# Short convolution in eight steps of sixteen channels, the skip term as a column, row pairs in the last product, and a new order of all work

## The chip, the cores and the metric

The kernel runs on one core of a Trainium2 chip. A core has five engines that work at the same time: TensorE (PE) multiplies matrices and writes the sums to PSUM, VectorE (DVE), ScalarE (ACT) and GpSimd (POOL) work on vectors, SyncE (SP) mostly issues transfers. They meet only at semaphores. PSUM has eight banks of 128 x 512 float32; whatever PE writes has to be moved to SBUF by DVE or ACT ("evacuated") before the bank can be used again.

The metric is the time of the program on the device in microseconds. A profiled execution gives a span, from the first to the last instruction, and its own time, which is a little longer.

## The reference, cut to what matters

Sequence S = 2048, width D = 640, hidden width F = 1728, all in bfloat16.

```
x  = A_q
q  = layernorm(x)
k_shift[s, d] = sum over t < 4 of k[s - t, d] * shift_k[d, t]      # short convolution
kv = k_shift * v
y  = causal_convolution(kv, ssm_k)                                # length S, by FFT
y  = y + kv * ssm_D                                               # skip term
h  = x + q * y
a  = mish(layernorm(h) @ w1 + b1)
h2 = h + a @ w2
```

The skip term is the same as adding ssm_D to the first tap of the long filter: the convolution with ssm_k[d, 0] + ssm_D[d] at lag 0 gives both.

## The kernel before, in words

**Tiling.** The 2048 positions lie as 128 partitions x 16 positions (p, t2) in memory; the long convolution is a transform written as matrix products. The width is cut into five blocks b of 128 channels, and these into chunks 0 (blocks 0, 1), 1 (blocks 2, 3) and 2 (block 4).

**Stages.** Names are those of the order list; a trailing x or y is the first or second half of a unit (one PSUM bank each).

- *k1pe/k1ev* (L625): the long filter ssm_k, loaded by channel rows into rn, is transposed block by block, 16 transposes each, and evacuated into kk_s. *dadd* (L620) then adds ssm_D to the first tap, which is 128 elements in one partition row; d_row is a row of ssm_D in the partition 0 of rn.
- *s1kpe/s1kev* (L543, L544): first transform of the filter. Cosine and sine products of 64 output rows each run on the two halves of the array's columns.
- *coef, wsh* (L487, L493, L501): the short filter. One matmul with a 0/1 matrix (rep4) copies shift_k to all partitions, four copies move it into coef with a shift per group of 32 partitions, and four products on POOL with a mask of 32 columns make banded matrices of 128 + 96 columns for each of 20 channel groups of 32.
- *ktpe/ktev* (L571): k is transposed, four channels groups by four time steps of 32 channels per unit; *ktsh* (L585) copies the last time group moved by one column.
- *kspe/kv* (L595, L596, L600): the short convolution. For each channel group and each group of four steps there are two products: 128 columns for the group itself and 96 for what the group before hands over. DVE multiplies the sum with v on the way out of PSUM.
- *s1vpe/s1vev*: first transform of kv, as for the filter.
- *s2kpe, s2vpe* (L652, L685): second transform, one matmul per frequency, with the table G (4 MB, eight loads d_g). Evacuated in place.
- *sw* (L668, L669): copies of the transformed filter with neighbouring partitions exchanged, in two halves of 64 frequencies per chunk; SP issues them.
- *p1, p2* (L706, L710): complex products of kv's and the filter's transforms, in quarters of 32 frequencies.
- *i1pe, i2p, y*: inverse transforms and their evacuation; *ln1, lnx, wb, h, bn, pow, hc*: the two layernorms and the gating; *trpe, trd*: transposes of the normalised rows.
- *m1pe* (L898), *hb* (L903): first product of the MLP in five units of 256, 256, 512, 512, 512 positions, 13 hidden blocks of 128, Mish on ACT. *m1pex* (L878): the last 64 hidden rows, two groups of positions on the two halves of the array, into the two halves of hbx.
- *m2pe* (L915, L916), *res* (L921), *d_out*: second product, 13 matmuls of 128 rows and a last one (L916) whose 128 rows hold the 64 of this group of positions and 64 that meet zeros (w2z and w2h_z, L760 and L761, write these zeros on POOL).
- *wm* and *fz* (L464, L468): matmuls on zeros, at the start and at four places later.

**Order.** ORDER lists all 1030 operations with their engine (t TensorE, a ScalarE, v VectorE, p GpSimd, d and s transfers issued by SP and ACT). _schedule walks this list, gives each operation a start by a cost model of its own and assigns PSUM banks; the program is emitted in the order of these starts. Each engine, and each queue of transfers, then works strictly in that order, and waits by semaphores where data or a buffer is missing. DVE and GpSimd products that use the same port are kept from overlapping in this plan, and a small copy (turn, L936) makes GpSimd wait where it follows DVE.

The functions the diff touches, and what calls them:

## Time and profile before

| | |
|---|---|
| three runs | 224.22, 224.60, 224.79 us, median 224.6 |
| profiled execution, own time | 224.86 us |
| its span | 223.1 us |
| granted TensorE clock | 1.00 |
| busy PE | 214.7 us (96%), 2598 matmuls |
| busy DVE, ACT, POOL | 146.2, 134.4, 65.7 us |
| DMA | 30.68 MB; 408 to 424 GB/s while the inputs load |

"Busy" of PE counts a matmul from its start to its modelled end; since matmuls are pipelined, a matmul of 128 columns counts about 0.22 us although the next can start 0.056 us later. So a busy share near 100% does not say that PE runs at its pace: that is read from how many matmuls start in a stretch. "Idle before" in a group's line is the time that an engine had nothing, with what ended it. A line such as L419 or L421 is the helper that all evacuations use.

### The profile page before, as it was taken

The numbers are of one execution on the slowest core, as the hardware profiler recorded it, in microseconds if no ns is written. First come the engines' busy times: TensorE is split into PE (matmuls) and PEld (weight loads), VectorE is DVE, ScalarE is ACT, GpSimd is POOL, SyncE is SP. The second block draws the span as 40 slices with busy tenths as digits, with TensorE's granted clock in tenths as the row PEclk, the third lists the DMA queues.
The fourth block names the chain that finished last, engine by engine and source line by source line (L and its number), as shares of the span: only waits on it lengthen the run. The fifth ranks groups of instructions, "written<-read, shape, count | busy, mean of one in ns | idle before, by whom it ended". The sixth has DMA issues, their size and how long they took to land.

```text
span 223.1 us, 6218 instructions
## 1 busy us (share of the span) xinstructions
PE 214.7 (96%) x2598; PEld 162.1 (73%) x2598; DVE 146.2 (66%) x317; ACT 134.4 (60%) x268; POOL 65.7 (29%) x106
## 2 busy tenths in 40 slices
PE   7998899999999999999999999999999999999994
PEld 2988899999877999988887644576645445675773
DVE  0699989999999998999788898974400000004023
ACT  2689989999999999888870446800053454330000
POOL 1271950005596007235767714320000000000000
PEclk9999999999999999999999999999999999999999
DMA  6999991075999999100001401043350000000024
GB/s 214 388 408 424 408 413 69 3 203 193 277 290 283 319 351 347 62 3 0 3 0 32 88 0 31 0 91 60 88 179 0 1 0 3 0 0 0 32 82 153
DMA packets 27342, 30.68 MB, mean 138 GB/s; under 512 B 9393, under 2 KB 23730, under 8 KB 26930
## 3 DMA queue, kind: packets, MB, share of 16 engines
q1 hardware_dynamic: 26880, 30.10, 41.1%
q8 instruction: 20, 0.33, 0.6%
q10 hardware_dynamic: 338, 0.18, 0.3%
q14 instruction: 8, 0.07, 0.1%
q0 software_dynamic: 96, 0.00, 0.0%
HBM read 20.45 MB, written 2.62 MB: 103 GB/s over the span
## 4 chain that ended last, share of the span: by engine, by line
PE 64%; DVE 13%; DMA 7%; ACT 7%; POOL 5%; issue 2%; SPq 0%; DVEq 0%; ACTq 0%; POOLq 0%
PE ps L915 21%; PE ps L898 19%; ACT uv L419 6%; DMA x<-in_A_q_dram 5%; PE ps L743 4%; PE ps L744 4%; PE ps L652 3%; PE ps L543 2%; PE ps L571 2%; DMA rn<-in_A_ssm_k_dram 2%; DVE st L776 2%; DVE st L822 2%; PE ps L595 2%; POOL r L782 2%; PE ps L916 2%
## 5 line engine op out<-in xcount | busy, mean ns | idle before, releaser
L915 PE MATMUL ps<-rn,uv 128*128 128x320 bf16 (+2 forms) x416 | 61.1, 299 | 0.2 <-DVE x L921 0.2
L903 ACT ACTIVATE uv<-ps,b1s 128x512 bf16<-128x512 f32 (+1 forms) x65 | 35.4, 610 | 39.1 <-PE ps L898 38.5
L898 PE MATMUL ps<-G 128*128 128x512 bf16 (+1 forms) x325 | 58.6, 337 | 0.0
L915 PEld LDWEIGHTS <-uv 128*128 128x128 bf16 x416 | 40.2, 98 | 17.5 <-issue 0.4
L419 ACT CAST uk<-ps 128x512 bf16<-128x512 f32 (+1 forms) x96 | 48.7, 702 | 2.6 <-PE ps L544 1.6
L898 PEld LDWEIGHTS <-G 128*128 128x128 bf16 x325 | 31.2, 98 | 23.9 <-issue 1.1
L921 DVE TENSOR_TENSOR xb<-ps,xb 128x320 bf16<-128x320 f32 (+2 forms) x12 | 5.7, 487 | 36.3 <-PE ps L916 35.8
L419 ACT CAST uv<-ps 128x512 bf16<-128x512 f32 (+2 forms) x57 | 28.7, 845 | 0.0
L921 DVE TENSOR_TENSOR xa<-ps,xa 128x320 bf16<-128x320 f32 x12 | 5.9, 488 | 21.6 <-PE ps L916 21.6
L827 POOL TENSOR_TENSOR r<-ve,mhalf 128x1 f32<-128x1 f32 x16 | 10.0, 630 | 32.7 <-DVE ve L824 32.7
L743 PE MATMUL ps<-a,uv 128*128 128x128 bf16 x160 | 18.8, 219 | 0.2
L421 DVE CAST uk<-ps 128x512 bf16<-128x512 f32 (+1 forms) x27 | 17.2, 669 | 1.4 <-PE ps L744 0.9
L743 PEld LDWEIGHTS <-uv 128*128 128x128 bf16 x160 | 17.9, 113 | 0.0
L421 DVE CAST uv<-ps 128x512 bf16<-128x512 f32 (+1 forms) x25 | 15.3, 677 | 0.0
L685 PE MATMUL ps<-uv,G 128*128 128x64 bf16 (+1 forms) x256 | 12.8, 197 | 0.8
L685 PEld LDWEIGHTS <-G 128*128 128x128 bf16 x256 | 11.1, 96 | 3.1 <-issue 2.1
L600 DVE TENSOR_TENSOR ra<-ps,rb 128x512 bf16<-128x512 f32 x20 | 12.5, 684 | 0.3 <-PE ps L596 0.3
L419 ACT CAST rb<-ps 128x512 bf16<-128x512 f32 (+1 forms) x28 | 10.6, 495 | 2.7 <-PE ps L803 2.7
L652 PE MATMUL ps<-uk,G 128*128 128x160 bf16 x128 | 12.1, 230 | 0.0
L782 POOL TENSOR_TENSOR r<-ve,mhalf 128x1 f32<-128x1 f32 x16 | 10.8, 672 | 1.3
L706 DVE TENSOR_TENSOR uv<-uv,uk 128x2048 bf16<-128x2048 bf16 (+1 forms) x11 | 10.9, 1022 | 0.0
L544 PE MATMUL ps<-cst,ra 128*64 128x128 bf16 x160 | 10.6, 220 | 0.1
(116 smaller groups left out, 376.7 us busy)
## 6 DMA issues: line engine op xcount, KB each, us to landing
G<-tab_g SPq DMA_DIRECT2D x8, 512.0 KB, 12.9
rn<-in_A_ssm_k_dram SPq DMA_DIRECT2D x5, 512.0 KB, 6.2
ra<-in_A_k_dram SPq DMA_DIRECT2D x4, 640.0 KB, 9.9
rb<-in_A_v_dram SPq DMA_DIRECT2D x2, 1280.0 KB, 13.1
G<-in_B_w_dram SPq DMA_DIRECT2D x5, 432.0 KB, 6.4
rn<-in_B_w_dram SPq DMA_DIRECT2D x1, 2080.0 KB, 9.8
rn<-uk SPq DMA_DIRECT2D x4, 512.0 KB, 5.1
rb<-uk SPq DMA_DIRECT2D x8, 256.0 KB, 7.9
```

The lines of the kernel that those rows point to most:

```text
L419: nc.scalar.copy(o, i)
L421: nc.vector.tensor_copy(o, i)
L600: nc.vector.tensor_tensor(kv_w[:, m, :, 8 * h:8 * h + 8, l0:l0 + n], ps.rearrange("p (l t d) -> p d t l", l=n, t=8), raw_v[:, 8 * h:8 * h ...
L652: nc.tensor.matmul(ps[:, o:o + 160], g_v[:, f, :], KA[:, :, f, :], start=True, stop=True)
L685: nc.tensor.matmul(ps[:, fl * n:fl * n + n], g_v[:, f0 + h * kf + fl, :], VX[x][:, :, f0 + h * kf + fl, :], start=True, stop=True)
L706: eng.tensor_tensor(v, v, K[c.i][:, :, f0:f1, :], ALU.mult)
L743: nc.tensor.matmul(pz[:, k, :], V[c.i][:, dg // 4, :, dg % 4], a12[:, 0, :], start=True, stop=False)
L782: nc.gpsimd.tensor_tensor(r1[:, t2:t2 + 1], ve1[:, t2:t2 + 1], mhalf[:, 0:1], ALU.pow)
L898: nc.tensor.matmul(ph[:, 0:w], w1[:, dc, fc * P:fc * P + P], lnhT_of(u)[:, dc, 0:w], start=(dc == 0), stop=(dc == NDC - 1))
L903: nc.scalar.activation(hb_of(u)[:, fc, 0:w], rt.tile[:, 0:w], ACT.Mish, bias=b1s[:, fc:fc + 1], scale=1.0)
L915: nc.tensor.matmul(po[:, 0:d1 - d0], hb_of(u)[:, fc, tl * P:(tl + 1) * P], w2[:, fc, d0:d1], start=(fc == 0), stop=False)
L921: nc.vector.tensor_tensor(x, rt.tile[:, 0:d1 - d0], x, ALU.add)
```

## The change

- **Short convolution.** Groups are now 16 channels by 8 time steps (128 rows again). A unit has the same eight matmuls, but the second of each pair has 48 columns, not 96; even and odd channels of a group of 32 go to every second column of the PSUM bank. The shifted coefficients are made by nine accumulating matmuls with parts of the identity as weights, evacuated by one copy on ACT; ten products on POOL, each 704 columns, make the banded matrices. The shift of the last time group is 8 x 127 elements instead of 4 x 127.
- **Skip term.** ssm_D comes as a column of five bfloat16 per partition (d_col): block 0 on ACT's queue, blocks 1 to 4 by four transfers of POOL. DVE adds a column of 128 x 1 to the raw filter (dq0 to dq4) ahead of the transposes of the first half. dadd and d_row are gone.
- **First filter block.** Its upper 64 rows are loaded by ACT, the lower by SP, and it is first. On ACT's queue the order is: half block, cst, d_col, sk_r.
- **Row pairs.** The last 64 rows of m2pe are a unit of their own, m2q: for two groups of positions and two parts of the output, products of 64 rows on the upper or the lower half of the array start the sums of four banks. The zeros (w2z, w2h_z) are gone. m1pex pairs the two halves of each unit.
- **Pieces.** The swap copies of chunk 0 go in four pieces of 32 frequencies, its products in eight of 16.
- **Fillers.** wm has eight matmuls, not nine; each fz two, not one, all four at places after the first transforms of v.
- **Order.** All 1052 operations stand in a new order. For PE it begins wm, k1pe0y, k1pe0x, cfpe, k1pe2y, k1pe2x, then s1kpe0. Loads are five filter blocks, k with d_x0 in it, a12, then v among the first table parts, then the rest of the table. In PE's order there are 58 changes between full-array matmuls and those on a half of it, where there were 28.

The core of the diff (the order list, constants of the planner and tile shapes are left out):

```diff
     def emit_act_dmas(e):
+        nc.scalar.dma_start(raw_n[0][64:P], n_view[0, 16:32])
         nc.scalar.dma_start(cst[:], dram["cst"])
-        nc.scalar.dma_start(sk_r[:], A_shift_k.rearrange("(d n) j -> d (n j)", n=20))
-        nc.scalar.dma_start(d_row, A_ssm_D.unsqueeze(0))
+        nc.scalar.dma_start(d_col[:, 0:1], d_view[0])
+        nc.scalar.dma_start(sk_r[:], A_shift_k.rearrange("(d n) j -> d (n j)", n=40))
+    def emit_dp(e):
+        for m in range(1, NDC):
+            nc.gpsimd.dma_start(d_col[:, m:m + 1], d_view[m])
...
-        nc.tensor.matmul(ps_f32(cf_rt)[:, 0:80], rep4, sk_r[:], start=True, stop=True)
+        ps = ps_f32(cf_rt)[:, 0:440]
+        for i, (a, j0, j1) in enumerate(((0, 0, 4), (4, 0, 4), (7, 1, 4), (7, 0, 1), (1, 0, 4), (2, 0, 4), (3, 0, 4), (5, 0, 4), (6, 0, 4))):
+            nc.tensor.matmul(ps.rearrange("p (r t) -> p r t", t=11)[:, :, a + j0:a + j1], cst[0:16, 3 * P - 16 * a:4 * P - 16 * a],
+                             sk_r[:].rearrange("p (r j) -> p r j", j=4)[:, :, j0:j1], start=(i == 0), stop=(i == 8))
...
-        for a in range(4):
-            ps = slice(a * 32, a * 32 + 32)
-            nc.vector.tensor_copy(coef[ps, :, a:a + 4], cf_rt.tile[ps, 0:80].rearrange("p (g j) -> p g j", j=4))
+        ev(e, coef[:], cf_rt.tile[:, 0:440])
...
-            nc.gpsimd.tensor_copy(t[:, :, 4, 1:128], t[:, :, 3, 0:127])
+            nc.gpsimd.tensor_copy(t[:, :, 2, 1:128], t[:, :, 1, 0:127])
...
-                for l in (2 * k, 2 * k + 1):
-                    r = 4 * m + l
-                    for a in (2 * h, 2 * h + 1):
-                        o = ps[:, (l - 2 * k) * 256 + (a - 2 * h) * P:][:, 0:P]
-                        nc.tensor.matmul(o, t[:, l, a, :], wsh[r // 5][:, r % 5, 0:128], start=True, stop=False)
-                        nc.tensor.matmul(o[:, 0:96], t[:, l, a - 1 if a else 4, :], wsh[r // 5][:, r % 5, 128:224], start=False, stop=True)
+                for l in range(2):
+                    for e in range(2):
+                        o, q, w = ps[:, 256 * l + e:256 * l + 256:2], 4 * e + 2 * k + l, wsh[m][k][:, e, l, :]
+                        nc.tensor.matmul(o, t[:, q, h, :], w[:, 0:128], start=True, stop=False)
+                        nc.tensor.matmul(o[:, 0:48], t[:, q, 0 if h else 2, :], w[:, 128:176], start=False, stop=True)
...
-        def dadd(e, kd=kd, rd=rd):
-            k = kd[0:1, 0]
-            (nc.vector if e == "dve" else nc.gpsimd).tensor_tensor(k, k, rd, ALU.add)
+        def dadd(e, n=n, b=b):
+            nc.vector.tensor_tensor(n[:, 0:1], n[:, 0:1], d_col[:, b:b + 1], ALU.add)
+        k1 = OP(f"dq{b}", ("dve", 0.1), [d_n[b], d_rows if b else d_row1], emit=dadd)
...
-        npf = (32, 32, 32)[len(c.dcs) - 1]
+        npf = (16, 32, 32)[c.i]
...
+            def pq(e, ab=ab, parts=parts):
+                for i in range(2):
+                    for t2 in ab:
+                        _, c, h = last64[t2]
+                        d0, d1, rt = parts[t2][i]
+                        rhs = w2h[64:P, d0:d1] if h else w2[0:64, 13, d0:d1]
+                        nc.tensor.matmul(ps_f32(rt)[:, 0:d1 - d0], hbx[64 * h:64 * h + 64, c:c + P], rhs, start=True, stop=False)
...
                     for fc in range(NFC - 1):
-                        nc.tensor.matmul(po[:, 0:d1 - d0], hb_of(u)[:, fc, tl * P:(tl + 1) * P], w2[:, fc, d0:d1], start=(fc == 0), stop=False)
-                    nc.tensor.matmul(po[:, 0:d1 - d0], lhs, w2h[:, d0:d1] if h else w2[:, 13, d0:d1], start=False, stop=True)
+                        nc.tensor.matmul(po[:, 0:d1 - d0], hb_of(u)[:, fc, tl * P:(tl + 1) * P], w2[:, fc, d0:d1], start=False, stop=(fc == NFC - 2))
```

More of the change, by code (lines that the diff above doesn't have):

```diff
@@ L187, in _schedule @@
         dur = dict(o.opts)[eng]
-        est = max([free.get(eng, 0.0)] + [d.finish + d.lat + _TAIL[d.eng] + _HOP for d in o.deps])
+        est = max([free.get(eng, 0.0)] + [d.finish + (0.0 if d.eng == eng and eng.startswith("dma") else d.lat + _TAIL[d.eng] + _HOP) for d in o.deps])
         base = est
@@ L191, in _schedule @@
             t, rt.slot = rt.ring.free()
+            rt.ring.take(rt.slot, rt)
             est = max(est, t)
@@ L204, in _schedule @@
                     t = fetched
-                fetched = t + (_SLOW if free.get("dma", 0.0) > t + 0.3 else _FETCH)
+                fetched = t + next(d for end, d in _FETCH if t < end)
                 mark += _BLOCK
@@ L215, in _schedule @@
                 o.behind = last
-        for rt in o.allocs:
-            rt.ring.take(rt.slot, rt)
         order.append(o)
@@ L327 @@
     turn = cpool.tile([P, 1], BF16, name="turn")
[L328 to L329 removed]
+    sk_r = cpool.tile([16, 160], BF16, name="sk_r")
+    d_col = cpool.tile([P, NDC], BF16, name="d_col")
+    coef = cpool.tile([P, 440], BF16, name="coef")
     st1 = cpool.tile([P, NT, 2, 6], F32, name="st1")
@@ L530 @@
     d_go = OP("d_go", ("dma", 0.75))
-    d_n = [DMA(f"d_n{b}", P * S * 2, emit_kn(b), deps=[d_go], lat=3.1) for b in range(NDC)]
+    d_n = [DMA("d_n0", P * S * 2, emit_kn(0), deps=[d_go], rate=405e3, lat=2.85)]
+    d_n += [DMA(f"d_n{b}", P * S * 2, emit_kn(b), deps=d_n[:1], rate=405e3, lat=3.2) for b in range(1, NDC)]
+    for o in d_k + d_v:
+        o.deps.append(d_n[0])
     s1_pes = [[] for _ in CHUNKS]
```

289 lines of the change are left out of this document (148 added, 141 removed).

## The prediction

> **What bounds the kernel now.** The profiled execution took 224.86 us around a span of 223.1 us; the median of the three runs is 224.6. I sum against 224.86 and take 0.26 off at the end.
>
> I read the table by stretches first: columns are the stretch, its length, busy us and instruction count of PE, PEld, DVE, ACT, POOL, then granted clock, DMA share, GB/s.
>
> ```profile
> 7.00:30.00 23.00, 21.10 (x489) 20.13 (x489) 20.98 (x43) 19.72 (x35) 14.26 (x18) 1.00 1.03 413
> 30.00:50.00 20.00, 20.00 (x420) 19.43 (x418) 19.95 (x34) 20.00 (x44) 1.49 (x3) 1.00 0.43 145
> 50.00:72.50 22.50, 20.95 (x464) 18.29 (x462) 22.34 (x32) 22.50 (x49) 14.94 (x9) 1.00 0.90 259
> 72.50:92.00 19.50, 19.41 (x319) 18.87 (x317) 17.70 (x31) 18.89 (x40) 4.67 (x8) 1.00 0.92 309
> 92.00:223.00 131.00, 127.82 (x895) 82.86 (x892) 64.67 (x178) 51.29 (x102) 29.31 (x58) 1.00 0.14 36
> ```
>
> There are two regimes. From 72.5 us on PE is never idle until the last outputs, and its matmuls come at a fixed pace: PE alone sets the end there. Before 72.5 us DVE and ACT are full (42.29 and 42.50 of 42.5 us from 30 on), because they empty PSUM; PE waits for them although it looks 95% busy, since a matmul's latency (about 0.2 us) covers the pauses. Between 7 and 30 us both evacuators have holes: 2.02 us on DVE, 3.28 on ACT, while the loads run at 413 GB/s.
>
> The chain of waits gives the paces and one pause of PE for "issue" (nothing that the profile shows):
>
> ```profile
> 26.93 0.83 issue
> 51.02 0.96 PE ps L685 x32
> 143.13 1.77 PE ps L915 x13
> 144.90 0.14 PE ps L916
> ```
>
> So a 320-column matmul costs 0.136 us and a 64-column one 0.03. The timeline of PE shows how much the pauses hide, what a short-convolution pair costs, and what a change of array form costs:
>
> ```profile
> 7.01 1.21 PE L625 MATMUL ps<-cst,rn 128*128 128x128 bf16 x16
> 8.15 0.24 PE L543 MATMUL ps<-cst,rb 128*64 128x128 bf16 x1
> 9.24 0.22 PE L544 MATMUL ps<-cst,rb 128*64 128x128 bf16 x1
> 9.39 3.23 PE L625 MATMUL ps<-cst,rn 128*128 128x128 bf16 x48
> 42.01 0.22 PE L595 MATMUL ps<-xb,uv 128*128 128x128 bf16 x1
> 42.06 0.20 PE L596 MATMUL ps<-xb,uv 128*128 128x96 bf16 x1
> 42.10 0.22 PE L595 MATMUL ps<-xb,uv 128*128 128x128 bf16 x1
> 60.65 2.51 PE L685 MATMUL ps<-uv,G 128*128 128x64 bf16 x56
> ```
>
> At 60.65 us 56 matmuls take 2.51 us where 0.03 each would be 1.68: PE waits for evacuated banks. A pair L595+L596 takes 0.10 us. From full-array to half-array matmuls (the last L625 starts at 7.01 + 1.21 - 0.22 = 8.00) and back (9.24 to 9.39) the step is 0.15 us instead of 0.06: about 0.1 us per switch, 0.11 with the slower first matmul behind it.
>
> The groups by shape (busy us, mean ns) give the prices off PE:
>
> ```profile
> L706 DVE TENSOR_TENSOR uv<-uv,uk 128x2048 bf16<-128x2048 bf16 x7 | 8.3, 1215 | 0.0
> L706 DVE TENSOR_TENSOR uv<-uv,uk 128x1024 bf16<-128x1024 bf16 x4 | 2.7, 685 | 0.0
> L493 DVE CAST coef<-ps 32x80 bf16<-32x80 f32 x4 | 1.0, 240 | 0.0
> L824 DVE TENSOR_SCALAR ve<-mv 128x1 f32<-128x1 f32 x16 | 2.5, 153 | 0.6
> L501 POOL TENSOR_TENSOR xb<-cst,coef 128x1120 bf16<-128x1120 bf16 x3 | 6.2, 2065 | 0.5 <-DVE coef L493 0.5
> L585 POOL COPY uv<-uv 128x508 bf16<-128x508 bf16 x5 | 3.0, 610 | 1.1 <-DVE uv L421 1.1
> ```
>
> **The change part by part.**
>
> *Evacuators (the bound before 72.5 us).* DVE loses the four coefficient casts (0.96), the memset of coef (0.18) and one skip add (0.21). Of the chunk-0 products it had six at 1.22 us (7.3); the new order has sixteen half-sized ones, nine on POOL, seven on DVE at 0.685 (4.8): -2.5. One chunk-2 product goes to POOL as well: -0.69. DVE gains five column adds, nearest row 0.15 each: +0.77. ACT gains one 440-column copy, about 0.5. The sum is -3.3 us over two engines that share this work, so **-1.6 us**. POOL does the moved products: ten at 2.05 (half of its 4.08 us for 2048) in a stretch where it now has 14.94 of 22.5 us busy and 1.49 of the 20 before. It is covered as long as POOL starts them near 45 us; without that cover DVE waits for POOL.
>
> *Late PE work (the bound behind 72.5 us).* The 32 last products of the down projection (L916 and its 512/128 forms) have a half of zeros; they become 32 of 64 rows. If each row pair runs at once, 16 x 0.136 = 2.2 us go. But eight such groups stand alone among full-array matmuls: 16 more switches at 0.11 = +1.8. Net **-0.4**. Not at once: +1.8. No row of this kernel has row pairs; the nearest are the column pairs L543/L544, whose two halves start 3 to 30 ns apart and step 0.055 us per pair, so I take "at once". The Trainium skill says the same of both forms (TensorE: Matmul & The Clock Gate, Part 3: tiles of different row groups overlap, starting some 4 ns apart); no run before the change shows it for rows. Cutting m1pex0 and m1pex2 into two narrower groups keeps their columns: 0. A group takes four of eight PSUM banks at once; the next one waits until four are free, covered by two 1.9 us matmul groups and DVE at 0.49 us a sum: 0, up to +0.5 without that cover.
>
> *Early PE work (beside the bound).* 80 second halves shrink from 96 to 48 columns: 0.042 to about 0.03, -1.0. Their outputs go to every second PSUM word, which no row shows: 0, at worst half speed (+4). The coefficients take nine matmuls of 160 columns at 0.07 instead of one: +0.5. One warm-up matmul fewer: -0.43; four fillers of two instead of one: +0.86. Switches in this part go from 22 to 36: +1.5. Together +1.4, hidden by the pauses of PE for the evacuators (0.83 us in the one L685 stretch above, more between 50 and 72.5): 0, +1.4 if the cover is gone.
>
> *Start.* The first filter block comes by two queues, and PE's first transposes wait for it and for cst. Before, its landing released PE at 5.71 us; now it may be near 5. But the x half waits for a column add, this for a 2-byte-element transfer (nearest: sk_r, 3.8 us to landing, here third on ACT's queue), and cfpe waits for sk_r as the fourth. Block 2's adds wait for POOL's four small transfers (b1b took 5.3 us to land), so about 7.5 us; the second block landed at 6.9. Better by 0.7 or worse by 0.6: I take 0.
>
> *POOL's early chain.* Ten coefficient products of 704 at 1.3 = 13.0 instead of 8.3, five shifts of 1016 at about 1.15 = 5.8 instead of 3.0. With coef at 11 us the shift for channel block 0 ends near 28; its matmuls come near 31 in the new order. Covered by 3 us.
>
> *Swap copies.* sw0 goes in four pieces with runs of 256 bytes instead of 512. Packets took 28 ns at 512 and 18 at 256 (output transposes), so 8192 x 18 / 16 = 9.2 us of the queues instead of 7.2: +2 us in a time that has 0.43 DMA share (30 to 50 us). Cost 0; at 28 ns a packet it is 14.3 us (rival 5).
>
> *The new total order.* SP now issues the five filter blocks, all of k, then v before most of the table: k is complete after 5.8 MB, at 400 GB/s from 3 us near 17.5 us, where the last k block landed at 21.6. So transposes and short convolution can fill the 2.0 and 3.3 us of holes in DVE and ACT, 2.65 in the mean. Between 0 and all I take half: **-1.3**. A new order can also open holes elsewhere; that is in the rivals.
>
> Sum: -1.6 - 0.4 - 1.3 = -3.3; 224.86 - 3.3 = 221.56, or 221.3 against the median.
>
> **Rivals.**
> 1. *The order is worth more.* All holes filled (-2.65), the 0.83 us of issue gone and the start earlier by 0.7: 224.6 - 1.6 - 0.4 - 2.65 - 0.8 - 0.7 = 218.5. For it: every part of it is seen as a hole. Against: the loads still end near 35 us.
> 2. *Slower: PE is the bound before 72.5 us too.* If PE's pauses there are smaller than the +1.4 us of switches, coefficients and fillers, evacuators that are free sooner give nothing: 224.6 + 1.4 - 0.4 = 225.6, with the start's 0.6 it is 226.2. It decides where less than 1.4 us of pauses remain in the new order. For it: 30 more switches. Against: 0.83 us of pause in one stretch of 2.5.
> 3. *Row pairs do not run at once.* 221.3 + 2.2 = 223.5.
> 4. *The moved products make POOL late.* POOL's 4.08 us per 2048 against DVE's 1.22; beside DVE products its small instructions already stretch. If chunk 0 ends about 3 us late, PE waits behind i1pe0 and all but the start's part of the gain goes: 224.3, no measurable change.
> 5. *A swap packet costs the same at 256 bytes.* Then sw0 fills the queues for 7.1 us more; the idle 6 us ahead of 43.7 us (SP's first swap issue) take some, and if 3 us of delay are left, the chunk-1 products and i1pe1 behind them wait: 224.3. Against: the 18 ns. The Trainium skill (DMA: Bandwidth & Descriptors, Specifications) speaks for this rival: under 512 bytes a transfer loses line rate to read-modify-write; the trace's 18 ns do not bear it out, though they are of another kind of copy.
>
> **How the numbers follow.** Forecast 0.46, rival 1 0.21, rival 2 0.19, rival 3 0.08, rival 4 0.04, rival 5 0.02. A difference under 0.3% (0.7 us) can hardly be told from none. Faster 0.46 + 0.21 + 0.08 = 0.75; same 0.04 + 0.02 = 0.06; slower 0.19. Range: from rival 1 less 0.7 for its own spread, 217.8, to rival 2 with the late start, 226.2. The forecast alone: 219.9 (all holes) to 222.6 (none).
>
> **What would show it.** Right: DVE and ACT full from about 10 us, PE's pauses between 50 and 72 us shorter, first i1 matmuls some 2 to 3 us earlier, and from there an unchanged pace with 0.27 us per row group plus two switches. Wrong: row halves 0.13 us apart; strided outputs above 0.056 us; PE's first half-array matmul later than 9 us; POOL products ending after DVE's; holes in ACT after 30 us.

## The result and the profile after

The changed kernel takes **235.73 us** (median of four runs, 235.47 to 235.93) where the kernel before, on the same chip, takes 224.66. The ratio is 1.050 (95% interval 1.048 to 1.052): 11.1 us slower, where 3.3 us faster was forecast, and far outside the range. The profiled span is 234.2 us against 223.1.

The table by stretches of the changed kernel (columns as before: the stretch, its length, busy us and instructions of PE, PEld, DVE, ACT, POOL, granted clock, DMA share, GB/s):

```profile
7.00:30.00 23.00, 20.06 (x336) 17.89 (x335) 13.22 (x27) 13.27 (x22) 9.56 (x13) 0.78 0.83 334
30.00:50.00 20.00, 20.00 (x414) 19.06 (x413) 18.03 (x33) 18.20 (x36) 14.95 (x24) 1.00 0.65 226
50.00:72.50 22.50, 22.32 (x461) 20.63 (x461) 20.43 (x35) 20.72 (x45) 16.81 (x8) 1.00 0.43 111
72.50:92.00 19.50, 18.30 (x321) 16.80 (x324) 18.52 (x28) 19.14 (x41) 4.55 (x4) 1.00 1.00 305
92.00:234.00 142.00, 138.34 (x1091) 91.40 (x1095) 74.41 (x199) 60.70 (x122) 33.64 (x64) 1.00 0.21 61
```

Two things have turned round. From 7 to 30 us PE runs 336 matmuls where it ran 489, and the evacuators DVE and ACT are busy 13.2 and 13.3 us where they had 21.0 and 19.7. From 30 to 72.5 us PE is the full engine (42.3 of 42.5) and the two evacuators have 4.0 and 3.6 us of holes; before it was the other way round.

Where the loss lies is read from the first matmuls of each stage. The first half-array matmul starts at 15.20 us, 7.05 later than before (8.15). The last half-array matmul of the first Fourier stage starts at 72.69, 12.4 later (60.32). The first L811 (the projection behind the gate) starts at 100.86, 12.0 later than its counterpart (88.87). From there to the end the changed kernel needs 133.3 us and the kernel before 134.2. So everything that is lost is lost before about 75 us: 7 us ahead of the first half-array matmul and about 5 between it and 75 us.

The chain of waits of the changed kernel begins so (start, us, what):

```profile
2.59 7.92 DMA d_col<-in_A_ssm_D_dram
10.86 1.08 PE ps L633 x8
11.94 1.48 PE ps L499 x9
13.41 1.86 PE ps L633 x16
18.40 1.16 PE ps L633 x16
```

The D column of the first filter block, 256 bytes, is on its way for 7.9 us; nothing useful is on the path until 10.86. Then 16 transposes take 1.86 us where 16 of the same take 1.16 five microseconds later: TensorE works at half pace. Its timeline shows the two pauses ahead of that (last bracket: idle time and what ended it):

```profile
8.50 1.01 PE L633 MATMUL ps<-cst,rn 128*128 128x128 bf16 x8 [3.66 <-DMA cst<-tab_cst]
10.86 1.08 PE L633 MATMUL ps<-cst,rn 128*128 128x128 bf16 x8 [1.35 <-DVE rn L627]
11.87 1.54 PE L499 MATMUL ps<-sk_r,cst 16*128 16x160 bf16 x9
13.35 1.92 PE L633 MATMUL ps<-cst,rn 128*128 128x128 bf16 x16
15.20 0.31 PE L558 MATMUL ps<-cst,xa 128*64 128x128 bf16 x1
```

The loads that these wait for (what is loaded and from where, queue, operation, KB, us from issue to landing), issued at 1.25, 1.96, 2.59 and 3.21 us:

```profile
rn<-in_A_ssm_k_dram ACTq DMA_DIRECT2D x1, 256.0 KB, 4.2
cst<-tab_cst ACTq DMA_DIRECT2D x1, 128.0 KB, 6.5
...
d_col<-in_A_ssm_D_dram ACTq DMA_DIRECT2D x1, 0.2 KB, 7.9
sk_r<-in_A_shift_k_dram ACTq DMA_DIRECT2D x1, 5.0 KB, 7.6
```

The identity lands at 8.45 us (before: 2.85), the column at 10.5 and the short filter at 10.8 (before: 4.9). They stand behind half a filter block on ScalarE's queue, and that queue began 0.5 us late, since a table load of ACT (0.72 to 2.00) was put ahead of it.

The short convolution's groups by shape, PE, of the kernel before (on its table tiles xb) and of the changed kernel (busy us, then ns of one):

```profile
L595 PE MATMUL ps<-xb,uv 128*128 128x128 bf16 x60 | 7.7, 218 | 0.0
L596 PE MATMUL ps<-xb,uv 128*128 128x96 bf16 x60 | 7.5, 205 | 0.0
```

```profile
L606 PE MATMUL ps<-xb,uv 128*128 128x128 bf16 x40 | 7.3, 284 | 0.0
L607 PE MATMUL ps<-xb,uv 128*128 128x48 bf16 x40 | 7.0, 248 | 0.0
```

A 128-column matmul was 218 ns long and is 284, a second half of 48 columns 248 where one of 96 was 205. By their starts (40.77, 40.85, 40.92, 41.00 ...) a pair takes 0.152 us, 0.098 before; for 80 pairs that is 4.3 us, in the stretch in which PE has now no slack. The stride alone costs more than that, since the second halves became shorter with the change: see the experiment with neighbouring words.

### The profile page after: what moved, and what is told of

It reads as the page before. It is cut to its first block, busy times and chain, and to the rows that moved or that the text cites. A ratio compares the mean times of both kernels' runs of the same rounds, so it can differ in the third digit from the quotient of the medians.

```text
span 234.2 us, 6332 instructions
## 1 busy us (share of the span) xinstructions
PE 222.6 (95%) x2619; PEld 166.9 (71%) x2629; DVE 145.0 (62%) x320; ACT 133.5 (57%) x263; POOL 82.1 (35%) x121
## 4 chain that ended last, share of the span: by engine, by line
PE 87%; DMA 5%; SPq 4%; ACT 2%; issue 1%; DVE 0%; ACTq 0%; DVEq 0%
PE ps L941 24%; PE ps L908 24%; PE ps L558 6%; PE ps L754 4%; PE ps L660 4%; PE ps L753 4%; PE ps L811 4%; PE ps L606 4%; DMA d_col<-in_A_ssm_D_dram 3%; PE ps L633 3%; PE ps L586 2%; SPq L676 2%; SPq L677 2%; PE ps L695 2%; PE ps L607 1%; ACT uk L420 1%
## 5 line engine op out<-in xcount | busy, mean ns | idle before, releaser
L941 PE MATMUL ps<-rn,uv 128*128 128x320 bf16 (+2 forms) x415 | 58.3, 299 | 0.1
L941 PEld LDWEIGHTS <-uv 128*128 128x128 bf16 x416 | 39.2, 98 | 18.3 <-issue 1.6
L420 ACT CAST uk<-ps 128x512 bf16<-128x512 f32 (+1 forms) x91 | 46.5, 630 | 5.8 <-PE ps L559 1.9
L422 DVE CAST uk<-ps 128x512 bf16<-128x512 f32 (+1 forms) x32 | 20.3, 666 | 2.4 <-PE ps L559 1.1
L835 POOL TENSOR_TENSOR r<-ve,mhalf 128x1 f32<-128x1 f32 x16 | 9.5, 596 | 30.9 <-DVE ve L832 28.1
L753 PEld LDWEIGHTS <-uv 128*128 128x128 bf16 x160 | 17.8, 113 | 0.1
L422 DVE CAST uv<-ps 128x512 bf16<-128x512 f32 (+1 forms) x23 | 14.2, 676 | 0.4 <-PE ps L695 0.3
L611 DVE TENSOR_TENSOR ra<-ps,rb 128x512 bf16<-128x512 f32 x20 | 13.2, 686 | 2.0 <-PE ps L607 1.6
L420 ACT CAST rb<-ps 128x512 bf16<-128x512 f32 (+1 forms) x26 | 10.5, 504 | 6.0 <-PE ps L811 6.0
L695 PE MATMUL ps<-uv,G 128*128 128x64 bf16 (+1 forms) x256 | 12.4, 198 | 1.0 <-ACT uv L420 0.8
L633 PE MATMUL ps<-cst,rn 128*128 128x128 bf16 x80 | 7.7, 263 | 5.0 <-DMA cst<-tab_cst 3.7
L513 POOL TENSOR_TENSOR xb<-cst,coef 128x704 bf16<-128x704 bf16 x5 | 6.8, 1365 | 15.0 <-DMA ra<-in_A_k_dram 15.0
L633 PEld LDWEIGHTS <-rn 128*128 128x128 bf16 x80 | 6.7, 156 | 6.7 <-issue 4.6
## 6 DMA issues: line engine op xcount, KB each, us to landing
rn<-in_B_w_dram SPq DMA_DIRECT2D x1, 2080.0 KB, 10.8
```

What stands on the lines that cost most here:

```text
L420: nc.scalar.copy(o, i)
L422: nc.vector.tensor_copy(o, i)
L611: nc.vector.tensor_tensor(kv_w[:, m, :, 8 * h:8 * h + 8, l0:l0 + n], ps.rearrange("p (l t d) -> p d t l", l=n, t=8), raw_v[:, 8 * h:8 * h ...
L633: nc.tensor.transpose(ps[:, t2, :], n[:, 8 * h + t2:S:16], ident)
L695: nc.tensor.matmul(ps[:, fl * n:fl * n + n], g_v[:, f0 + h * kf + fl, :], VX[x][:, :, f0 + h * kf + fl, :], start=True, stop=True)
L753: nc.tensor.matmul(pz[:, k, :], V[c.i][:, dg // 4, :, dg % 4], a12[:, 0, :], start=True, stop=False)
```

## The experiments

### The start: what the small loads wait behind

Issue order alone (ScalarE's loads ahead of its table load), in the changed kernel:

```
-... d_dr:s d_n0:d d_n2:d d_dp:p d_id:s d_sk:s wm:t ...
+... d_id:s d_dr:s d_n0:d d_n2:d d_dp:p d_sk:s wm:t ...
```

> The changed kernel with one swap in the order list: ACT issues its four transfers ahead of the load of its activation table, as the kernel before did, not behind it. If the start is lost because these transfers are issued late (1.25 to 3.2 us instead of 0.72 to 1.6), cst, behind the half filter block, lands 0.5 us sooner or much more, and the time falls by 0.5 to 3 us, to 233 to 235. If it is lost because cst and the small transfers stand behind the half block and beside SP's blocks, it falls by no more than 0.6 us. If the start does not matter (the loss is in the order behind it), nothing changes: 235.7.

Measured: 234.41 us, ratio to before 1.042 (1.036 to 1.047). Between 1.3 us (by the medians) and 1.8 (by the ratios) of 11. The identity lands 2.4 us sooner (6.0), the column and the short filter hardly (10.1 and 10.3), and the first half-array matmul starts at 14.8.

The same, and the whole first filter block on SP's queue, so that ScalarE's carries the three small loads alone:

```
-        nc.scalar.dma_start(raw_n[0][64:P], n_view[0, 16:32])
...
-        return lambda: nc.sync.dma_start(raw_n[b], n_view[b]) if b else nc.sync.dma_start(raw_n[0][0:64], n_view[0, 0:16])
+        return lambda: nc.sync.dma_start(raw_n[b], n_view[b])
```

> The changed kernel with the start of the kernel before: the whole first filter block on SP's queue, and cst, the skip column and the short filter on ACT's queue with nothing in front of them. Theory of the start: cst by 3 us, the column by 5, the first half-array matmul at 8 to 9 us instead of 15.2, granted clock 1.0 from 5 us on, and 6 to 7 us less: 229 to 230. Rival, more work on PE and a worse order behind it: the seven us are made up by later waits anyway and the time falls by less than 2 us, to 234 or more.

Measured: 228.68 us, ratio 1.018 (1.012 to 1.024); **7.0 us** of the loss are gone. The DMA issues of this kernel:

```profile
cst<-tab_cst ACTq DMA_DIRECT2D x1, 128.0 KB, 2.2
...
d_col<-in_A_ssm_D_dram ACTq DMA_DIRECT2D x1, 0.2 KB, 3.9
sk_r<-in_A_shift_k_dram ACTq DMA_DIRECT2D x1, 5.0 KB, 5.2
```

Issued at 0.72, 1.11 and 1.86 us, they land at 2.9, 5.0 and 7.0. The first half-array matmul starts at 9.0, and PE runs at full pace.

More warm-up matmuls in the changed kernel (24, not 8), to carry the pace over the pause:

```
-        for _ in range(8):
+        for _ in range(24):
```

> The changed kernel with 24 warm-up matmuls instead of 8, which keep PE busy until just before cst lands; nothing else. It parts the start's loss in two: waiting (unchanged here: first transposes at 8.5 us, the column at 10.7) and the half clock between about 8 and 18 us. If the half clock costs what its matmuls show, about 3 us (from 10.9 to 18 us at half pace), the time is 232 to 233; if the loads would have held PE anyway, 235 or more.

Measured: 234.82 us in the median, with executions from 232.8 to 236.0. In the profiled one (232.76) the matmuls kept full pace: 16 transposes step 0.062 us and not 0.107, and the first half-array matmul started at 13.4. So the half pace costs up to 3 us where it falls away, and the repair doesn't hold in each execution: only one execution has a trace, and what the others did stays open.

Is it the half block by itself? The kernel before, with that part alone (its first block is block 2):

```
     def emit_act_dmas(e):
+        nc.scalar.dma_start(raw_n[2][64:P], n_view[2, 16:32])
         nc.scalar.dma_start(cst[:], dram["cst"])
...
-        return lambda: nc.sync.dma_start(raw_n[b], A_ssm_k.rearrange(...)[b])
+        return lambda: nc.sync.dma_start(raw_n[2][0:64], n_view[2, 0:16]) if b == 2 else nc.sync.dma_start(raw_n[b], n_view[b])
```

> The kernel before with one part of the change alone: the upper half of the filter block that it loads first goes out on ScalarE's queue ahead of the table with the identity, the short filter and the D row. Theory (the small loads land behind the half block whatever else the kernel does): identity lands near 6 us and not 2.9, the short filter and the D row at 7 to 11 us and not near 5; first half-array matmul at 11 to 15 us and not 8.15; 228 to 232 us. Rival (the late start needed POOL's D column pieces or the new order): within 1 us of the kernel before, 224 to 226.

Measured: 225.25 us, ratio 1.003 (1.002 to 1.005). My theory in this form fell: the identity lands near 6 us there too, but the short filter at 7.2, and the first half-array matmul at 8.8. Half a microsecond, not six.

What else does the changed start have? The column ahead of the half block on ScalarE's queue (issue order as in the first edit):

```
     def emit_act_dmas(e):
+        nc.scalar.dma_start(d_col[:, 0:1], d_view[0])
         nc.scalar.dma_start(raw_n[0][64:P], n_view[0, 16:32])
         nc.scalar.dma_start(cst[:], dram["cst"])
-        nc.scalar.dma_start(d_col[:, 0:1], d_view[0])
```

> The changed kernel with ScalarE's loads issued first, and among them the first D column (128 pieces of 2 bytes) ahead of the half filter block, not behind it. Theory (the half block alone cost the kernel before 0.5 us; what costs 6 us is the D column landing at 10 us, on which the column add, the second half of the transposes and then half the TensorE pace hang): column lands before 6 us, first half-array matmul near 9.5 us, about 229.5 us (228.5 to 231). Rival (the half block delays the identity and the short filter just as much, and they hold the start): 233 to 235, as with the issue order alone.

Measured: 234.69 us, ratio 1.044 (1.041 to 1.047), nothing gained; again the theory fell. The column lands at 2.9, but now the identity lands at 9.2 and PE pauses 4.4 us for it.

POOL's four column loads (128 pieces of 2 bytes each) as the suspect: on the kernel before, into a tile that nothing reads, with the half block and without:

```
+        for m in range(1, NDC):
+            nc.gpsimd.dma_start(spare[:, m:m + 1], A_ssm_D.rearrange("(d m l) -> m d l", m=NDC, l=4)[m])
```

> The kernel before with the half filter block on ScalarE's queue and, in addition, the four D column loads of 128 x 2 bytes issued by POOL at the start, into a tile that nothing reads. Theory (POOL's column loads hold the DMA engines back between 6 and 9 us, where all kernels that have them move 195 to 290 GB/s and those without 390 to 420; loads behind the half block fall into that): the cost of the half block rises from 0.5 us to several, 227.5 to 231 us, with the 6 to 9 us rate below 300 GB/s. Rival (the column loads matter only as data: the column add waits for them): as the half block alone, 224.8 to 225.8.

> The kernel before with only POOL's four D column loads added, nothing reading them. Theory (they cost only what lands while they run): the rate falls between 6 and 9 us, but the small loads have landed before 5 us; 0.3 to 1.0 us more than the kernel before, 224.9 to 225.7. Rival (no contention): 224.3 to 224.9.

Measured: 226.40 us, ratio 1.008 (1.005 to 1.011), with the half block, and 225.05, ratio 1.002 (1.001 to 1.004), without. The stretch from 6 to 9 us, first of the kernel before with the half block, then of the one with the columns too:

```profile
6.00:9.00 3.00, 2.59 (x39) 2.29 (x40) 0.89 (x3) 1.59 (x2) 0.00 (x0) 1.00 1.03 406
```

```profile
6.00:9.00 3.00, 2.06 (x26) 1.82 (x26) 0.81 (x2) 1.01 (x1) 0.00 (x0) 0.95 0.85 305
```

The column loads do slow the others (406 to 305 GB/s), and the two together cost more (1.8 us) than one by one (0.5 each). But 1.8 is not 6. In the changed kernel, the columns taken from POOL to the end of ScalarE's queue, once with the half block and the issue order of the first edit, once in the kernel with both repairs (below):

```
-            nc.gpsimd.dma_start(d_col[:, m:m + 1], d_view[m])
+            nc.scalar.dma_start(d_col[:, m:m + 1], d_view[m])
```

> The changed kernel with ScalarE's loads issued first and the four other D columns taken from POOL's queue to the end of ScalarE's; the half block stays ahead of the small loads. Theory (POOL's loads are what turns the half block's 0.5 us into 6): rate at 6 to 9 us back near 400 GB/s, column and short filter land by 7.5 us, first half-array matmul near 10 us, 229 to 231 us. Rival (it is the half block with 128-piece columns behind it on the same queue): 233.5 to 235.5.

> The kernel with both repairs (224.28) with the four other D columns taken from POOL's queue to ScalarE's. Theory (POOL's loads cost this start the 0.6 us by which its first half-array matmul is later than before): 0.3 to 0.8 us less, 223.5 to 224.0, faster than the kernel before. Rival (their landing has no one waiting here): 224.1 to 224.6.

Measured: 233.12 us, ratio 1.038 (1.035 to 1.040), and 224.96, ratio 1.002 (1.000 to 1.003). The first is 1.3 us better by the medians than with the issue order alone (0.9 by the ratios), not 4; the second is no better than on POOL's queue (ratio 0.999). In both, SP's own queue stands for a filter block in this time (4.9 and 3.1 us), which the other kernels don't show so long; why is not settled. Taken from POOL's queue, the columns give back about 1 us of the 7.

What is left are the waits that only the changed kernel has at its start. Both edits start from the issue order of the first experiment. The D term of the first block left out, so that nothing waits for the column; then, in addition, the nine coefficient matmuls moved behind the third block's transposes, so that nothing waits for the short filter:

```
-            nc.vector.tensor_tensor(n[:, 0:1], n[:, 0:1], d_col[:, b:b + 1], ALU.add)
+            if b:
+                nc.vector.tensor_tensor(n[:, 0:1], n[:, 0:1], d_col[:, b:b + 1], ALU.add)
```

```
-... k1pe0x:t cfpe:t warm:a ... coef:a s1kev2_0y:a k1pe1x:t k1pe1y:t k1ev1x:a ...
+... k1pe0x:t warm:a ... s1kev2_0y:a k1pe1x:t k1pe1y:t cfpe:t k1ev1x:a coef:a ...
```

> The changed kernel with ScalarE's loads issued first and the addition of D to the first filter block left out (the D term of the first of five blocks is missing), so that the second half of its transposes waits for no column. Theory (the start hangs on whichever of the small loads lands last behind the half block; the nine coefficient matmuls stand in front of the next transposes and wait for the short filter, which lands at about the same 10 us): second transposes at 7 us, then TensorE stands until the short filter has landed near 10 us; 232.5 to 234.5. Rival (it is the column alone): 228.5 to 230.5.

> As the run before, and the nine coefficient matmuls moved behind the third filter block's transposes, so that the start waits neither for the column nor for the short filter; half block, POOL's column loads and order otherwise as in the changed kernel. Theory: identity at 6 us, no pause of 3 us on TensorE and so no half pace, first half-array matmul at 8.5 to 10 us, 228 to 229.5, as with the small loads ahead of the block (228.7). Rival (the half block slows the filter blocks themselves, and they hold the start): above 231.

Measured: 234.45 us, ratio 1.044 (1.039 to 1.048), and 231.80, ratio 1.031 (1.025 to 1.036). PE's waits up to 22 us, first without the wait for the column, then without both (engine, tile, line, what was waited for, total, times, longest):

```profile
PE ps L499 <- DMA sk_r<-in_A_shift_k_dram: 3.0, 1, 3.0
PE ps L634 <- DMA cst<-tab_cst: 1.0, 1, 1.0
```

```profile
PE ps L634 <- DMA rn<-in_A_ssm_k_dram: 2.4, 1, 2.4
PE ps L634 <- DMA cst<-tab_cst: 1.2, 1, 1.2
```

So **the start has no single late load**. With the wait for the column gone, PE stands 3.0 us for the short filter; with that gone too, 2.4 us for the second filter block. TensorE runs at half pace for a part of the start in both (transposes at 0.107 us a step: without the column's wait from 5.9 us on, ahead of the 3.0 us wait; with both waits gone from 9.6 to 15.3 us). The first half-array matmul comes at 14.8, 14.1, 11.5 as the waits go, and at 9.0 with the whole block on SP's queue. Of the expected 228 to 229.5 only half was gained. That fits the rival, that the half block holds the filter blocks themselves back, but doesn't settle it: the trace without both waits is that of the slowest of its executions, and with the same loads the second filter block landed at 7.4 us with the issue order alone, at 8.2 without the wait for the column, and at 9.5 here. What is shown is that the whole block on SP's queue takes the loss away; how the loss divides among the loads and the half pace is not.

### The outputs to every second PSUM word

The coefficient products of the changed kernel written to neighbouring words, sixteen channels together, and the product with v reading them in that order:

```
-                        o, q, w = ps[:, 256 * l + e:256 * l + 256:2], ...
+                        o, q, w = ps[:, 256 * l + 128 * e:256 * l + 128 * e + 128], ...
...
-                nc.vector.tensor_tensor(kv_w[...], ps.rearrange("p (l t d) -> p d t l", l=n, t=8), ...
+                u = lambda x: x.rearrange("p (d e) t l -> p d e t l", e=2)
+                nc.vector.tensor_tensor(u(kv_w[...]), ps.rearrange("p (l e t d) -> p d e t l", l=n, e=2, t=8), ...
```

> The changed kernel with one thing changed in the short convolution: the two 16-channel groups write neighbouring PSUM columns (128 in a row) instead of every second column, and the multiplication by v reads them apart. If every second column is what makes a pair of 128 and 48 columns take 0.152 us (0.098 before with 128 and 96), the pair falls to about 0.085 and, with PE the bound there, the time by 4 to 5.4 us, to 230.3 to 231.7. If the weights or the short second matmul are what is slow, the pair stays at 0.15 and the time at 235.7. If the pair falls and the time does not, PE is not the bound in that stage.

Measured: 232.06 us, ratio 1.029 (1.024 to 1.035): 3.7 us less by the medians, 4.5 by the ratios (1.050 less 1.029 of 224.7). The groups that answer to those above:

```profile
L606 PE MATMUL ps<-xb,uv 128*128 128x128 bf16 x40 | 4.6, 216 | 0.0
L607 PE MATMUL ps<-xb,uv 128*128 128x48 bf16 x40 | 4.3, 183 | 0.0
```

The 128-column matmuls have their old length again, those of 48 columns are 183 ns long, and DVE's product with v does not suffer (0.686 us before the repair, 0.681 to 0.683 in the kernels with it). A pair steps 0.081 us now, so the stride cost 0.071 a pair, 5.7 us of PE's time for 80; against the kernel before it is 4.3, since the second halves shrank (1.4). From the first transpose of a k block to the first L811 the traces give 75.6 us with strided outputs and 71.5 without, 4.1 less, and 76.05 and 71.51, 4.5 less, once the start is repaired. So 5.7 us of PE's work cost 4.1 to 4.5 us of time; the rest lay in pauses. The start is the same in the two kernels (first half-array matmul at 15.2 and 15.5, TensorE at half pace in both).

Both repairs together:

> The changed kernel with both repairs: the whole first filter block on SP's queue with only the three small loads on ScalarE's, and the coefficient products written to neighbouring PSUM words. Theory: the late start and the strided outputs are the whole loss and add, 228.7 - 3.7 = 225.0 us (224.0 to 226.0), that is, equal to the kernel before within 0.6%. Rival (the new order costs something of its own, hidden so far under a TensorE that bounded 30 to 72 us): above 226.5. Second rival (the evacuators' savings of my forecast, 1.6 us, and the order's 1.3 come out once nothing lies over them): 221 to 223.

Measured: **224.28 us**, ratio 0.999 (0.997 to 1.001): as fast as the kernel before and no faster. So 7.0 us are the start, 4.3 the strided outputs (1.018 to 0.999), and all other parts of the change together come to nothing measurable in the whole time, where I had forecast -3.3. In the two profiled executions, the first half-array matmul comes 0.6 us later than before (8.72), from there to the first L811 it is 0.6 less (80.1 against 80.7), and from there to the end 0.9 less (133.3 against 134.2): the late gain is there, while what the earlier parts save is no more than the late start. Its table by stretches:

```profile
7.00:30.00 23.00, 22.73 (x498) 20.77 (x496) 19.18 (x40) 20.80 (x37) 14.74 (x23) 1.00 1.00 406
30.00:50.00 20.00, 19.44 (x453) 18.59 (x450) 19.76 (x34) 19.50 (x43) 16.53 (x19) 1.00 0.49 158
50.00:72.50 22.50, 21.50 (x445) 18.46 (x444) 22.24 (x36) 22.50 (x49) 12.30 (x7) 1.00 0.91 245
72.50:92.00 19.50, 19.50 (x313) 18.96 (x311) 17.36 (x32) 18.74 (x39) 6.10 (x9) 1.00 0.71 257
```

### Where the forecast gain went

The evacuators did get less work: up to 92 us DVE and ACT together are busy 163.0 us, 164.6 in the kernel before, so 0.8 us less each (forecast 1.6). But the holes between 7 and 30 us did not fill: by the first line of the table they are 6.0 us for the two together (3.8 and 2.2), by that of the kernel before 5.3 (2.0 and 3.3). 4.6 of the 6.0 now lie between 7 and 18 us, where PE is busy 10.99 of 11.00 us. From 72.5 to 92 us PE is full (19.50) as it was. To see which side sets the pace between, work was added to the evacuators of the kernel with both repairs (64 columns copied twice in 40 evacuations), and taken from PE (four filler matmuls less, and the nine coefficient matmuls later):

```
                 ev(e, (V, K)[which][c.i][:, b0:b0 + n, :, :], ps.rearrange("p (b g f) -> p b f g", b=n, g=4))
+                if not which:
+                    ev(e, V[c.i][:, b0:b0 + n, 0:16, :], ps.rearrange(...)[:, :, 0:16, :])
```

> From the kernel with both repairs: each of the 40 evacuations of the value half of the first Fourier stage copies 64 of its columns a second time, 40 small operations on VectorE and ScalarE between 41 and 70 us, by the rows of other small operations 0.1 to 0.25 us each, 2 to 4 us more per engine. Strided outputs put 4.3 us on TensorE between 28 and 63 us and cost 4.4. Theory (TensorE and the two evacuators are balanced there, so that work added to either side shows in full and work taken from one shows in part at most): 80 to 100% of the added time per engine, 226.0 to 228.2. Rival (TensorE alone bounds that stretch): under 1 us, 224.3 to 225.2.

```
-... [nc.tensor.matmul(ps_f32(rt), wz[:, 0:P], wz[:, P:D], ...) for _ in range(2)])
+... [nc.tensor.matmul(ps_f32(rt), wz[:, 0:P], wz[:, P:D], ...) for _ in range(1)])
...
-... k1pe0x:t cfpe:t warm:a ... coef:a s1kev2_0y:a k1pe1x:t k1pe1y:t k1ev1x:a ...
+... k1pe0x:t warm:a ... s1kev2_0y:a k1pe1x:t k1pe1y:t cfpe:t k1ev1x:a coef:a ...
```

> From the kernel with both repairs, less TensorE work: each filler op has one matmul and not two (0.86 us less between 60 and 70 us), and the nine coefficient matmuls come after the third filter block's transposes, so that the first half-array matmul starts 0.8 us sooner. Theory (TensorE and evacuators balanced): half of it shows, 223.4 to 224.0. Rival 1 (TensorE alone is the bound): 222.8 to 223.4. Rival 2 (the fillers and the nine matmuls lie in pauses): 224.3, no change.

Measured: 231.59 us (ratio 1.033, 1.029 to 1.037) with the added copies, and 225.11 (1.003, 1.001 to 1.006) with less on PE. The copies put 5.3 us on ACT and 3.4 on DVE, 4.3 in the mean, and cost 7.3. Part of this lies at the start of the profiled execution: TensorE ran at half pace from 7.6 to 11 us, and the first transpose of a k block came 1.5 us late (18.80 against 17.32). From there to the first L811, in which stretch all copies lie, it is 77.5 us against 71.5: 6.0 more, still more than the copies put on either engine. The stretch from 40 to 72.5 us, with the copies:

```profile
40.00:72.50 32.50, 28.04 (x593) 24.00 (x588) 30.00 (x60) 31.78 (x82) 19.05 (x14) 1.00 0.59 155
```

PE falls to 28.0 of 32.5 us (31.2 without the copies), and DVE too has pauses: in an order that is fixed instruction by instruction each engine waits for the other. So work added to the evacuators showed in full and more, and of work added to PE (the strided outputs, 5.7 us) some three quarters. The kernel with 0.86 us less on PE is no faster (0.8 us slower by the medians): from the first transpose of a k block to the first L811 it takes 71.4 us against 71.5, so those fillers lay in pauses. Its moved coefficient matmuls brought the first half-array matmul only 0.25 us forward, where 0.8 was expected, and the first transpose of a k block came 0.6 later. This fits evacuators that set the pace between 18 and 72 us, with 1.2 to 1.6 us of slack on PE, as the prediction had it; a saving on the evacuators alone was not tried.

### The row halves of the last product

The kernel with both repairs, the four matmuls of a group tile by tile, and then all four on the lower 64 rows:

```
-                for i in range(2):
-                    for t2 in ab:
+                for t2 in ab:
+                    for i in range(2):
```

> As the kernel with both repairs, but the four half-array matmuls of a pair of row tiles of the second MLP product are issued tile by tile (lower, lower, upper, upper) and not in turn, so that only the two in the middle can run at once. Theory (the halves run at once, 0.143 us a step, TensorE sets the end there): a group takes three steps and not two, 8 x 0.143 = 1.1 us more than the kernel with both repairs. Rival (the halves do not run at once, or TensorE has slack there): 0 to 0.3 more.

```
-                        rhs = w2h[64:P, d0:d1] if h else w2[0:64, 13, d0:d1]
-                        nc.tensor.matmul(..., hbx[64 * h:64 * h + 64, c:c + P], rhs, ...)
+                        rhs = w2[0:64, 13, d0:d1]
+                        nc.tensor.matmul(..., hbx[0:64, c:c + P], rhs, ...)
```

> From the kernel with both repairs: all four half-array matmuls of a group read the lower 64 rows (the upper tiles' part of the sum over the last 64 hidden columns is left out). In the run with the pairs apart a group still took 0.477 us and not 0.59. Theory (a matmul over 64 rows takes half a step whichever rows it reads, so that two of them cost one full one): the group stays at 0.47 to 0.48 us with starts 3 to 7, 140 and 3 to 7 ns apart. Rival (two can only run at once on different halves, and the order in the run before was not what it seemed): four starts some 136 ns apart, 0.73 us a group, 8 x 0.26 = 2.1 us more in the stage.

Measured: 224.40 us (1.002, 0.999 to 1.005) with the order turned, no loss in the late stage (133.4 us from the first L811 to the end, 133.3 with pairs); and 226.84, one run, with all on one half, where that stage takes 135.5. The timelines of a group, of the changed kernel, of the turned order, and of the one half:

```profile
124.66 0.31 PE L929 MATMUL ps<-rn,hbx 64*128 64x320 bf16 x1
124.67 0.31 PE L929 MATMUL ps<-w2h,hbx 64*128 64x320 bf16 x1
124.81 0.30 PE L929 MATMUL ps<-rn,hbx 64*128 64x320 bf16 x1
124.81 0.30 PE L929 MATMUL ps<-w2h,hbx 64*128 64x320 bf16 x1
125.04 0.50 PE L908 MATMUL ps<-G 128*128 128x256 bf16 x3
```

```profile
113.05 0.31 PE L929 MATMUL ps<-rn,hbx 64*128 64x320 bf16 x1
113.06 0.31 PE L929 MATMUL ps<-w2h,hbx 64*128 64x320 bf16 x1
113.20 0.30 PE L929 MATMUL ps<-rn,hbx 64*128 64x320 bf16 x1
113.21 0.30 PE L929 MATMUL ps<-w2h,hbx 64*128 64x320 bf16 x1
113.43 0.28 PE L908 MATMUL ps<-G 128*128 128x256 bf16 x1
```

```profile
113.37 0.71 PE L929 MATMUL ps<-rn,hbx 64*128 64x320 bf16 x4
114.02 0.39 PE L908 MATMUL ps<-G 128*128 128x256 bf16 x2
```

On different halves, two matmuls start 3 ns apart and a group takes 0.38 us to the next full-array matmul; on one half they follow each other and it takes 0.65, eight times 0.27 or 2.2 us. My second theory (64 rows at half price whichever they are) fell, the pairs are real. In the turned order the program lists rn, rn, w2h, w2h (rn holds the lower weights, w2h the upper), and the starts show rn, w2h, rn, w2h: the first matmul of the upper half went ahead of the second of the lower. The text ahead of the prediction has each engine work strictly in its order; for these two it did not hold.

## Why the prediction was wrong, point by point

- **"Start: better by 0.7 or worse by 0.6: I take 0."** This step failed by 7.0 us. I priced the small loads by how long one took before (3.8 us, alone on its queue with two others), and did not ask what stands ahead of them now: half a filter block on the same queue. They took 6.5 to 7.9 us. I also gave no price to TensorE's half pace, though the warm-up matmuls in front of it hint at one. The sign "first half-array matmul later than 9 us" was the right one to look for: 15.2.
- **"Outputs to every second PSUM word: 0, at worst half speed (+4)."** The mechanism was named and the wrong end taken. The pair takes 0.152 us, 0.098 before and 0.081 with neighbouring words: 5.7 us of PE's work against a bound of 4, and 4.3 us against the kernel before. No row showed it, and between ends of 0 and 4 a value in between would have been due.
- **"Hidden by the pauses of PE for the evacuators: 0, +1.4 if the cover is gone."** The cover was enough for the 1.4 but thin: in the kernel with both repairs, taking 0.86 us of it away changed nothing, and PE's slack there is 1.2 to 1.6 us. With the stride's 5.7 us more PE had no pause left: the case of rival 2, by a load on PE that the rival did not have.
- **"Evacuators -1.6 us."** Half right in busy time (0.8 us each up to 92 us), wrong as a saving: with both defects repaired the time to the first L811 is the same as before (88.83 and 88.87 us).
- **"The new total order: -1.3."** Not seen. Half of the holes of 5.3 us were to be filled; in the repaired kernel they are 6.0, most of them before 18 us, where PE is full. PE as the bound, the picture of rival 2, holds in this stretch of the repaired kernel, not behind it.
- **"Late PE work: -0.4."** Right: row pairs run at once, switches are 0.09 to 0.10 us, a group is 0.48 us with both of them against four times 0.136 before; 0.5 us by the groups, 0.9 by the stage (133.3 us from the first L811 to the end, 134.2 before). Rival 3 is excluded.
- **POOL and the swap copies.** Right to take at nothing: the moved products took 2.13 us each (forecast 2.05), the longest wait of DVE for them was 0.7 us in the repaired kernel, and the pieces of 256-byte runs landed 3.0 to 5.7 us after their issue. Rival 4 is excluded, and the premise of rival 5 too: a packet of 256 bytes took 18 ns, one of 512 took 27 to 28. The rule of the Trainium skill that I cited there (DMA: Bandwidth & Descriptors, Specifications), of line rate lost under 512 bytes, agrees in its direction with these copies inside SBUF (14 bytes a ns at 256, 18 at 512), but the loss is small: a packet of half the size takes two thirds of the time.

In the changed kernel itself SP stood 14.8 us for the last transform of one filter block before it could issue the first v load; in the kernel with the start repaired it is 7.7 us and the transfers already issued cover it, so I take it for a consequence of the start. That was not tried by itself.

## What to carry to other kernels

A small load's time to land belongs to its place, not to its size: before moving a large transfer onto a queue, list everything that is queued behind it and who waits for each, since taking away one late load only brings the next one to light. When two engines are both full, price a saving on one of them at nothing until the trace shows that the other has slack; work added to the fuller one counted in full here. Where a layout that no row shows is given to TensorE's outputs, one small run of that layout tells more than any bound.

## What the runs showed of the hardware

- Matmuls whose outputs went to every second 4-byte word of PSUM were 284 ns long instead of 216 for 128 columns, 248 instead of 183 for 48, and a pair stepped 0.152 us; with neighbouring words a pair stepped 0.081 us, and writing to them brought the time back.
- In many kernels TensorE's matmuls stepped at 0.107 us at the start where 0.062 is usual. After pauses of 2.4 to 4.4 us (five kernels) this lasted 5.7 to 11 us, with PE busy for most of that time (7.65 of 9 us below). But the length of the pause doesn't decide: in the kernel with the added copies the half pace came at 7.6 us behind pauses of 0.5 us at most, and a pause of 1.2 us was followed by 0.062 us in two kernels. What sets it off stays open. The Trainium skill (TensorE: Matmul & The Clock Gate, Part 1) puts the return to half rate at one idle window of about 3.4 us and the full rate after about as long of sustained work; the factor of two agrees, while the slow stretch here is about two to three times as long, and began in some kernels without such a pause. The granted clock does not always tell: from 9 to 18 us it reads 0.50 in the changed kernel and 1.00 in the one with neighbouring words, whose transposes step at 0.107 in that time as well; that trace has its first record of the clock only at 19.5 us, so the 1.00 is no reading.

The stretch from 9 to 18 us, of the changed kernel and of the one with neighbouring words:

```profile
9.00:18.00 9.00, 7.65 (x92) 6.72 (x92) 2.43 (x8) 3.51 (x5) 0.00 (x0) 0.50 1.02 419
```

```profile
9.00:18.00 9.00, 7.51 (x87) 6.58 (x87) 2.17 (x6) 3.25 (x5) 0.00 (x0) 1.00 1.02 418
```

- With row halves listed lower, lower, upper, upper, the starts show lower, upper, lower, upper, 6 or 7 ns and 140 ns apart, and the second to start carries the wait on the upper half's weights that the third in the list has. So a matmul for the idle half went ahead of an earlier one for the busy half. The Trainium skill (TensorE: Matmul & The Clock Gate, Part 3) has matmuls start strictly in program order; this trace differs.
- Four loads of 128 pieces of 2 bytes, one kilobyte in all, went with a fall of the transfer rate from 406 to 305 GB/s over 3 us (the two rows of 6 to 9 us above).
